# One pitch of 512 values for VectorE's exponential and term tiles, five resident w2 parts, and an order computed for loads that land later

## The chip, the cores and the metric

One core of one Trainium2 chip runs the kernel. Its time is the device time of one execution in microseconds (us). Below, PE is TensorE, DVE is VectorE, ACT is ScalarE, POOL is GpSimd and SP is SyncE, whose only work here is to issue DMAs.

## The reference

Softcap attention over 8 batches, 12 heads, 448 positions and 64 values per head is followed by a soft mixture of experts (MoE) with 8 experts of 4 slots each:

```
scores = cap * tanh((q @ k.T / 8) / cap)            # cap = 30
attn   = exp(scores - max); attn /= sum + 1e-9
x      = attn @ v  -> [3584, 768]
logits = x @ phi                                     # 32 slots
d = softmax over tokens, c = softmax over slots
slot_out[e] = relu((d.T @ x)[e] @ w1[e]) @ w2[e]     # 768 -> 1024 -> 768
out    = c @ slot_out                                # float32
```

## The kernel before

**Quads.** The 96 heads are taken four at a time, as 24 "quads"; three quads make a batch. A quad Q has 14 score tiles of 128 keys by 448 queries. They are made in six chunks of 3, 2, 3, 2, 2, 2 tiles. `SC(Q,s)` are the PE matmuls of chunk s into one of two PSUM buffers (a ring: the even chunks use the 3-bank buffer, the odd ones the 2-bank buffer). `TH(Q,s)` is the tanh of that chunk on ACT (line 526), from PSUM into SBUF. So `SC(Q,s)` can begin only when `TH` of two chunks before has read the buffer.

**Two ways to the exponential.** Tiles 0 to 7 go into `exa`; `EX(Q,0)` takes their exponential on ACT in one instruction (line 534). Tiles 8 to 13 go into `exd`; DVE makes their exponential from four integer passes `PH(Q,0..3)` (function `term`, line 541), each of which reads the tanh values as float16 and writes a bfloat16 bit pattern as uint16. The first three passes write to one of two `term` buffers in turn, the fourth writes in place to `exd`. PE adds the four patterns up by multiplying each with its own V: `PV(Q,a0)`, `PV(Q,a1)` and `PV(Q,d)` are the products with `exa`, `PV(Q,c0)` to `PV(Q,c3)` those with the four passes (function `pv_mms`, line 551).

**Around them.** `NR(Q,0)` and `NR(Q,1)` divide by the row sums on DVE (lines 584 and 585). `TX`/`CX` turn the result on PE and copy it on DVE. `T k`/`T q` turn the keys and queries on PE, `C k`/`C q` copy them on DVE. Keys arrive as float32 by SP's queue (`LK`, line 407) and are cast on DVE (`KC`, line 411). Values arrive by SP's queue in four pieces (`LV`, line 417), are cast on POOL (`VC`, line 422) and scaled on DVE (`VS`, line 425). Queries are cast in the load by POOL's queue (`L q`, line 402). Once a batch, PE makes the MoE's logits and slot sums (`LG`, `SS`, `EN`, `ET`, `ES`), with small steps on the other engines (`EE` on ACT; `ED`, `ER` on POOL; `CS`, `CE`, `CN`, `CW` on DVE).

**What sets the order.** The class `Plan` lists all these steps with an engine, a duration from the table `COST`, dependencies and a due time. The due times are moved by the table `DUE`, and `HOLD` lets a step be picked although it isn't ready for up to so many ns. `Plan.order` then plays the engines forward and writes out the order in which each engine's instructions are emitted. The engines run them in that order and wait on semaphores; nothing is reordered on the chip. In the plan a load counts as landed `COST["dma"]` ns after its transfer ends.

**The layout.** A tile of `exa` has 448 values at a pitch of `ROW` = 512. `exd` and the `term` buffers keep their six tiles in three pairs: 512 values to the second tile of a pair, and `PAIR` = 960 from one pair to the next (function `pairs`), so that one strip of 64 zeros serves both tiles of a pair. A DVE pass over six tiles therefore walks 3 pairs of 2 tiles of 448 values.

**The end.** After the attention the MoE's second layer reads w2 in 32 parts of 384 KB. `KEPT` of them stay in SBUF in bfloat16 (`w2b`). The others are cast during the attention by POOL's queue into DRAM (`w2d`, line 335) and read back by SP's queue (`w2t`, line 868) into the SBUF that the attention gives up. Matmuls of line 922 use them, line 889 is the first layer.

Of the kernel before, what the change touches and what calls it, by code (L numbers as in the profile page):

```python
# [10 lines left out]
BF16 = mybir.dt.bfloat16  # L11
U16 = mybir.dt.uint16
# [5 lines left out]
P = 128  # L18
# [3 lines left out]
S = 448  # L22
# [3 lines left out]
W = DH + 1  # L26
SLOTS = 8
ROW = 512
PAIR = ROW + S


TILES = [(0, 0, 0), (0, 1, 0), (0, None, None), (0, 0, 1), (0, 1, 1), (0, 0, 2), (0, 1, 2),
# [5 lines left out]
RQ = 2  # L38
RP = 2
ND = 6  # L40
NA = NQT - ND
# [4 lines left out]
TERMS = ((-2.18104, 1.0), (-1.928978, 1.0), (-1.674805, 0.6953125), (-1.419015, 0.6953125))  # L46
PH = len(TERMS)

DUE = {"C0k": -134148, "C0q": -266909, "CAk": -221411, "CAq": -170905, "CE": -35220, "CN": -341840, "CS": -94513,
# [7 lines left out]
HOLD = {"C0k": 61, "C0q": 1500, "CAq": 1040, "CS": 7, "CW": 892, "Ck": 1367, "Cq": 775, "ED": 657, "EE": 1500, "ET":  # L57
# [4 lines left out]
COST = dict(quad=9000, lat=200, dma=5000, form=90, sc=100, scm=200, act=0.833, act0=70, ts=0.265, ts0=70,  # L62
            pvf=31, turn=460, xturn=450, copy=610, norm=830, vcast=1060, vscale=340, kcast=560, kdiag=300,
            issue=800, load=1400, part1=2740, part2=2530, same=300)

# [1 line left out]
class Plan:  # L67
# [5 lines left out]
    def op(self, name, eng, dur, deps=(), due=0.0, take=None, give=None, after=0.0, form=(FULL, FULL), port=False):  # L73
        key = name[0] + (str(name[2]) if name[0] in ("PV", "NR", "PH", "EX", "LG", "SS") else "") + \
            (name[1] if name[0] in ("L", "X", "T", "C", "CA", "T0", "C0") else "")
        self.ops[name] = dict(name=name, eng=eng, dur=dur, deps=list(deps), due=due + DUE.get(key, 0.0),
                              key=key, hold=max(0, HOLD.get(key, 0)), take=take, give=give, after=after, form=form, port=port)

    def build(self):
        C, NQ, NQB = COST, self.NQ, self.NQB  # L80
        T = float(C["quad"])
# [108 lines left out]
    def order(self):  # L190

        ops, lat = self.ops, COST["lat"]
        engines = ("PE", "ACT", "DVE", "POOL", "SP", "DMA", "DMV")
# [8 lines left out]
        def ready(o):  # L202
            t = o["after"]
            for d in o["deps"]:
                if d not in end:
                    return None
                x = ops[d]["eng"]
                t = max(t, end[d] + (0 if x == o["eng"] else COST["dma"] if x[0:2] == "DM" else lat))
            if o["take"]:
# [5 lines left out]
        while len(end) < len(ops):  # L215
            best = None
            for e in engines:
                pick = None
                for o in todo[e][:1 if e in strict else 60]:
                    r = ready(o)  # L220
                    if r is None:
                        continue
                    late = o["due"] - (COST["same"] if e == "PE" and o["form"][0] == form else 0)
                    key = (max(r - o["hold"], free[e]), late, str(o["name"]), max(r, free[e]))
# [7 lines left out]
            if e == "PE":  # L232
                if o["form"][0] != form:
                    t = max(t, free[e] + COST["form"])
                form = o["form"][1]
# [16 lines left out]
def kernel(  # L252
# [23 lines left out]
    NQB = H // 4  # L276
    NQ = B * NQB
    NPAIR = 2 * NQ
    KEPT = 6

    ctx.enter_context(tc.manual_schedule())
    pe, dve, act, pool, sp = nc.tensor, nc.vector, nc.scalar, nc.gpsimd, nc.sync
# [30 lines left out]
           for e in range(E - 2)]  # L313
    w2b = wts.tile([P, KEPT, 4, HD], BF16, name="w2b")

# [23 lines left out]
    w2_parts = [(n0, half) for n0 in range(0, len(blocks), 4) for half in range(2)]  # L339
    w2_kept, w2_spilled = w2_parts[:KEPT], w2_parts[KEPT:]  # L340

# [7 lines left out]
    homes = {}  # L349
# [2 lines left out]
        homes[nm] = att.enter_context(tc.tile_pool(name=nm, bufs=1))  # L352
    xs = att.enter_context(tc.tile_pool(name="xs", bufs=4))
    ea = [homes[f"ea{n}"].tile([P, NA * ROW], BF16, name=f"exa{n}") for n in range(RQ)]
    ed = [homes[f"ed{n}"].tile([P, ND // 2 * PAIR], BF16, name=f"exd{n}") for n in range(RQ)]
    terms_of = [homes["tm"].tile([P, ND // 2 * PAIR], BF16, name=f"term{n}") for n in range(RP)]
    kraw = [homes["ld"].tile([P, 2, S], F32, name=f"kraw{n}") for n in range(2)]
    kcast = homes["ld"].tile([P, 2, S], BF16, name="kcast")
    vraw = [homes[f"vr{n}"].tile([P, 2, SLOTS, DH], F32, name=f"vraw{n}") for n in range(2)]
# [4 lines left out]
    def rows(t):  # L364
        return t.rearrange("p (t s) -> p t s", s=ROW)

    def pairs(t, u0, u1):

        return bass.AP(tensor=t.tensor, offset=t.offset + u0 // 2 * PAIR,
                       ap=[t.ap[0], *([[PAIR, (u1 - u0) // 2]] if u1 - u0 > 2 else []), [ROW, 2], [1, S]])  # L370

    for t in ea:
        dve.memset(rows(t)[:, :, S:ROW], 0.0)
    for t in (*ed, *terms_of):
        dve.memset(t.rearrange("p (t s) -> p t s", s=PAIR)[:, :, S:ROW], 0.0)
    for t in km:
        dve.memset(t, 0.0)
    w_low = TERMS[-1][1]
# [138 lines left out]


    def quad_ex(Q, u0, u1):
        if u1 <= NA:  # L520
            return rows(ea[Q % RQ])[:, u0:u1, 0:S]
        return pairs(ed[Q % RQ], u0 - NA, u1 - NA)

    def tanh_chunk(Q, s):
        u0, w = first_of[s], CHUNKS[s]
        act.activation(quad_ex(Q, u0, u0 + w).bitcast(F16), ring(Q, s)[:, 0:w, 0:S], ACT.Tanh,  # L526
                       scale=qk_scale / cap)

    def nd_of(Q):
        return ND_LAST if Q == NQ - 1 else ND  # L530
# [5 lines left out]
    def term_home(Q, i):  # L536
        return ed[Q % RQ] if i == PH - 1 else terms_of[(Q * (PH - 1) + i) % RP]

    def term(Q, i):
        nd = nd_of(Q)  # L540
        dve.tensor_scalar(pairs(term_home(Q, i), 0, nd).bitcast(U16),  # L541
                          quad_ex(Q, NA, NA + nd).bitcast(F16), octaves * 128, base[i], ALU.mult, ALU.add)

    def pv_mms(dst, buf, vt, tiles, begin=False, end=False):
        for g in range(NG):
            for x in tiles:
                n, a, t = TILES[x]
                for h in range(2) if a is None else (a,):
                    q0 = x * ROW if x < NA else (x - NA) // 2 * PAIR + (x - NA) % 2 * ROW
                    q0 += (g * P if not h else g * P + HP if g < NF else -HP)  # L550
                    pe.matmul(dst[:, 2 * g + h if g < NF else 2 * g, :], buf[:, q0:q0 + P],  # L551
                              vt[:, 3 + h if a is None else 5 * h + t, :],
                              start=begin, stop=end, skip_group_check=True)
                    begin = False
# [175 lines left out]
    t = wts.tile([P, 2, 2, NT, DH], BF16, name="casts", tag="w1", bufs=E)  # L730
# [32 lines left out]
    Q, bl = NQ - 1, B - 1  # L763
# [102 lines left out]
    for n0, half in sorted(w2_spilled, key=lambda x: (x[1], x[0])):  # L866
        t = tl.tile([P, 4, HD], BF16, name=f"w2t{n0}_{half}")
# [195 lines left out]
```

## Time and profile before

| what | us |
|---|---|
| median of 3 runs (302.5 to 304.14) | 303.12 |
| the profiled execution | 302.8 |
| its span, first to last instruction | 301.0 |
| PE, DVE, ACT busy in the span | 255.5, 242.0, 236.9 |
| POOL busy in the span | 99.1 |

A busy time is the union of an engine's instructions; those of neighbours overlap a little at their ends, so the distance between two starts is shorter than a duration. The attention runs to about 256 us, the experts and the output fill the rest.

### The profile page before, as it was taken

What the parts mean: (1) busy time and instruction counts of PE and PEld (TensorE: products, weight loads), DVE (VectorE), ACT (ScalarE), POOL (GpSimd) and SP (SyncE); (2) the same over time, 40 slices, a digit from 0 to 9 for tenths busy, and PEclk for the clock granted to TensorE, in tenths of its full rate; (3) what the DMA queues carried; (4) which work ended last, traced back from release to release, by engine and by line L of the source; (5) the groups of instructions that cost most, each with busy time, mean ns of one, the idle gap of its engine ahead of it and who ended that gap; (6) DMA issues with size and microseconds to landing.
All of it is one profiled execution on the core that took longest, in us unless ns stands there. A gap on an engine that the chain in (4) does not pass through costs nothing.

```text
span 301.0 us, 11981 instructions
## 1 busy us (share of the span) xinstructions
PE 255.5 (85%) x5300; PEld 188.4 (63%) x5300; DVE 242.0 (80%) x437; ACT 236.9 (79%) x207; POOL 99.1 (33%) x156
## 2 busy tenths in 40 slices
PE   4879898999898969998988899879998999998720
PEld 4357577776676758776766676668666867543300
DVE  2459898999989989999989999799989987236940
ACT  1788979999899879998988898898989896235730
POOL 3570442633352324343524341624343210300000
PEclk9999999999999999999999999999999999999995
DMA  8999999999999999999999999999989998968998
GB/s 147 271 219 222 254 255 231 250 249 244 245 239 242 245 248 240 231 229 234 233 221 191 225 208 236 160 212 227 208 185 227 233 307 285 399 264 298 404 412 332
DMA packets 58931, 74.97 MB, mean 249 GB/s; under 512 B 4864, under 2 KB 48000, under 8 KB 58880
## 3 DMA queue, kind: packets, MB, share of 16 engines
q0 software_dynamic: 30464, 30.50, 62.3%
q1 hardware_dynamic: 28256, 43.49, 44.8%
q8 instruction: 41, 0.67, 0.8%
q10 hardware_dynamic: 160, 0.23, 0.3%
q14 instruction: 10, 0.08, 0.1%
HBM read 93.68 MB, written 21.23 MB: 382 GB/s over the span
## 4 chain that ended last, share of the span: by engine, by line
PE 33%; DVE 30%; DMA 19%; issue 5%; ACT 4%; SPq 3%; POOL 1%; DVEq 0%; ACTq 0%; POOLq 0%
PE pv L551 13%; DVE term L541 12%; DMA vraw<-in_v_dram 10%; DMA kraw<-in_k_dram 5%; DVE exd L541 5%; PE sc L515 4%; DVE vw L425 3%; SPq L417 3%; DVE xq L585 3%; PE xps L596 2%; DVE kcast L411 2%; PE hp L889 2%; PE so_ps L922 2%; DMA qb<-in_q_dram 2%; PE qps L482 2%
## 5 line engine op out<-in xcount | busy, mean ns | idle before, releaser
L526 ACT ACTIVATE exa<-sc 128x1344 f16<-128x1344 f32 (+1 forms) x72 | 82.3, 1166 | 20.0 <-PE sc L512 17.4
L541 DVE TENSOR_SCALAR term<-exd 128x2688 uint16<-128x2688 f16 (+1 forms) x72 | 76.0, 1081 | 2.0 <-PE pv L551 1.1
L534 ACT ACTIVATE exa<-exa 128x3584 bf16<-128x3584 f16 x24 | 76.7, 3195 | 0.0
L526 ACT ACTIVATE exd<-sc 128x896 f16<-128x896 f32 x72 | 63.5, 918 | 5.7 <-PE sc L515 5.6
L551 PEld LDWEIGHTS <-term 128*128 128x128 bf16 x1704 | 57.5, 97 | 12.6 <-DVE term L541 7.1
L515 PE MATMUL sc<-qT,kT 64*128 64x448 bf16 x288 | 50.0, 368 | 1.9 <-ACT exa L526 1.4
L422 POOL CAST vb<-vraw 128x1024 bf16<-128x1024 f32 x24 | 25.6, 1067 | 63.8 <-PE pv L551 36.3
L551 PE MATMUL pv<-vb,term 128*128 128x65 bf16 x1136 | 43.1, 193 | 1.5 <-DVE term L541 1.2
L551 PE MATMUL pv<-vb,exa 128*128 128x65 bf16 x960 | 41.9, 196 | 1.4 <-issue 1.1
L551 PEld LDWEIGHTS <-exa 128*128 128x128 bf16 x960 | 36.3, 99 | 9.4 <-issue 6.1
L541 DVE TENSOR_SCALAR exd<-exd 128x2688 uint16<-128x2688 f16 (+1 forms) x24 | 31.0, 1290 | 0.8
L585 DVE TENSOR_TENSOR xq<-pv,rec 128x448 bf16<-128x448 f32 (+2 forms) x49 | 30.1, 615 | 1.7
L551 PE MATMUL pv<-vw,exd 128*128 128x65 bf16 x568 | 22.1, 194 | 10.6 <-DVE exd L541 8.0
L402 POOL DMA_DIRECT2D qb<-in_q_dram x23 | 16.9, 736 | 42.2 <-PE qps L482 42.2
L551 PEld LDWEIGHTS <-exd 128*128 128x128 bf16 x576 | 19.2, 97 | 13.2 <-DVE exd L541 9.8
L551 PE MATMUL pv<-vw,term 128*128 128x65 bf16 x568 | 21.8, 193 | 4.0 <-DVE term L541 3.6
L491 DVE COPY qT<-qps 128x896 bf16<-128x896 bf16 x23 | 14.2, 617 | 7.3 <-PE qps L482 6.5
L335 POOL DMA_DIRECT2D w2d<-in_moe_w_dram x26 | 19.7, 790 | 0.5 <-issue 0.5
L515 PEld LDWEIGHTS <-kT 64*128 64x128 bf16 x288 | 12.9, 93 | 10.8 <-issue 3.6
L637 POOL COPY e<-E 128x512 bf16<-128x512 bf16 x9 | 5.8, 644 | 38.8 <-PE eps L655 17.8
L331 POOL DMA_DIRECT2D w1b<-in_moe_w_dram x24 | 18.1, 756 | 0.0
L512 PE MATMUL sc<-qT,km 128*128 128x448 bf16 x48 | 18.0, 375 | 0.0
(135 smaller groups left out, 315.1 us busy)
## 6 DMA issues: line engine op xcount, KB each, us to landing
w1b<-in_moe_w_dram POOLq DMA_DIRECT2D x24, 512.0 KB, 12.1
kraw<-in_k_dram SPq DMA_DIRECT2D x23, 448.0 KB, 9.0
w2d<-in_moe_w_dram POOLq DMA_DIRECT2D x26, 384.0 KB, 9.3
w2t<-w2d SPq DMA_DIRECT2D x26, 384.0 KB, 7.4
out_dram<-ob SPq DMA_DIRECT2D x9, 768.0 KB, 6.7
vraw<-in_v_dram SPq DMA_DIRECT2D x48, 128.0 KB, 7.1
qb<-in_q_dram POOLq DMA_DIRECT2D x23, 224.0 KB, 6.7
vraw<-in_v_dram SPq DMA_DIRECT2D x48, 96.0 KB, 7.4
```

The lines of the kernel that those rows point to most:

```text
L331: pool.dma_start(out=w1b[e][:, js, :], in_=w1r[:, e, js, :])
L335: pool.dma_start(out=dst, in_=bass.AP(tensor=src.tensor, offset=src.offset + half * HD, ap=[[D, P], [F * D, 4], [1, HD]]))
L402: pool.dma_start(out=t, in_=bass.AP(tensor=srcs[nm].tensor, offset=quad_at(Q), ap=[[NT * DH, P], [2 * S * DH, 2], [1, NT * DH]]))
L422: pool.tensor_copy(vb[Q % 2][:, :, :, 0:DH], vraw[Q % 2])
L491: dve.tensor_copy(new_qkT(nm, Q), ps)
L512: pe.matmul(dst, km[Q % 2][:, n, :], qT, start=True, stop=True)
L515: pe.matmul(dst, kT[r, 2 * t:2 * t + 2, :], qT[r], start=True, stop=True)
L526: act.activation(quad_ex(Q, u0, u0 + w).bitcast(F16), ring(Q, s)[:, 0:w, 0:S], ACT.Tanh, scale=qk_scale / cap)
L534: act.activation(t, t.bitcast(F16), ACT.Exp, scale=cap)
L541: dve.tensor_scalar(pairs(term_home(Q, i), 0, nd).bitcast(U16), quad_ex(Q, NA, NA + nd).bitcast(F16), octaves * 128, base[i], ALU.mult, AL ...
L551: pe.matmul(dst[:, 2 * g + h if g < NF else 2 * g, :], buf[:, q0:q0 + P], vt[:, 3 + h if a is None else 5 * h + t, :], start=begin, stop=e ...
L585: dve.tensor_tensor(xq[Q][:, s0:s1, n, :], ps[:, s0:s1, 0:DH], rec.to_broadcast([P, s1 - s0, DH]), op=ALU.mult)
```

## The change

The six tiles of `exd` and of the `term` buffers now lie at one pitch of 512, like those of `exa`; `pairs` and `PAIR` are gone. The buffers grow from 2880 to 3072 values per partition. In return w2 keeps five parts instead of six, and 27 instead of 26 are written to DRAM and read back. `COST["dma"]` becomes 7000 instead of 5000, and `DUE` and `HOLD` have new numbers (a line of each is shown), so every engine's order is computed anew.

```diff
-DUE = {"C0k": -134148, "C0q": -266909, "CAk": -221411, "CAq": -170905, "CE": -35220, "CN": -341840, "CS": -94513,
+DUE = {"C0k": -50327, "C0q": -3265, "CAk": -29335, "CAq": -19945, "CE": -129605, "CN": 17674, "CS": -25093, "CW":
...
-HOLD = {"C0k": 61, "C0q": 1500, "CAq": 1040, "CS": 7, "CW": 892, "Ck": 1367, "Cq": 775, "ED": 657, "EE": 1500, "ET":
+HOLD = {"C0k": 688, "C0q": 1260, "CAq": 1250, "CS": 998, "CW": 685, "CX": 544, "Ck": 509, "Cq": 1290, "ED": 1500,
...
-COST = dict(quad=9000, lat=200, dma=5000, form=90, sc=100, scm=200, act=0.833, act0=70, ts=0.265, ts0=70,
+COST = dict(quad=9000, lat=200, dma=7000, form=90, sc=100, scm=200, act=0.833, act0=70, ts=0.265, ts0=70,
...
-    KEPT = 6
+    KEPT = 5
...
-    ed = [homes[f"ed{n}"].tile([P, ND // 2 * PAIR], BF16, name=f"exd{n}") for n in range(RQ)]
-    terms_of = [homes["tm"].tile([P, ND // 2 * PAIR], BF16, name=f"term{n}") for n in range(RP)]
+    ed = [homes[f"ed{n}"].tile([P, ND * ROW], BF16, name=f"exd{n}") for n in range(RQ)]
+    terms_of = [homes["tm"].tile([P, ND * ROW], BF16, name=f"term{n}") for n in range(RP)]
...
-    for t in ea:
+    for t in (*ea, *ed, *terms_of):
         dve.memset(rows(t)[:, :, S:ROW], 0.0)
-    for t in (*ed, *terms_of):
-        dve.memset(t.rearrange("p (t s) -> p t s", s=PAIR)[:, :, S:ROW], 0.0)
...
     def quad_ex(Q, u0, u1):
-        if u1 <= NA:
-            return rows(ea[Q % RQ])[:, u0:u1, 0:S]
-        return pairs(ed[Q % RQ], u0 - NA, u1 - NA)
+        t, at = (ea, 0) if u1 <= NA else (ed, NA)
+        return rows(t[Q % RQ])[:, u0 - at:u1 - at, 0:S]
...
-        dve.tensor_scalar(pairs(term_home(Q, i), 0, nd).bitcast(U16),
+        dve.tensor_scalar(rows(term_home(Q, i))[:, 0:nd, 0:S].bitcast(U16),
...
-                    q0 = x * ROW if x < NA else (x - NA) // 2 * PAIR + (x - NA) % 2 * ROW
+                    q0 = (x if x < NA else x - NA) * ROW
```

ACT, one quad in the middle of the attention, before (`exa<-sc` and `exd<-sc` are tanh chunks, `exa<-exa` is the exponential):

```order
L526 ACTIVATE exa_161<-sc_192 128x2x448
L526 ACTIVATE exa_161<-sc_191 128x3x448
L526 ACTIVATE exd_163<-sc_192 128x2x448
L534 ACTIVATE exa_161<-exa_161 128x8x448
L526 ACTIVATE exd_163<-sc_191 128x2x448
L526 ACTIVATE exd_163<-sc_192 128x2x448
```

ACT at the same place now:

```order
L517 ACTIVATE exa_162<-sc_193 128x2x448
L517 ACTIVATE exa_162<-sc_192 128x3x448
L517 ACTIVATE exd_164<-sc_193 128x2x448
L517 ACTIVATE exd_164<-sc_192 128x2x448
L525 ACTIVATE exa_162<-exa_162 128x8x448
L517 ACTIVATE exd_164<-sc_193 128x2x448
```

The exponential has moved behind the fifth tanh chunk, so that one chunk is left behind it instead of two.

DVE, the four passes over `exd` of one quad and what stands around them, before (`term<-exd` and `exd<-exd` are `PH`, `rec` and `xq` are `NR`, `kT` and `km` are `C k`, `qT` is `C q`, `xT` is `CX`, `vw` is `VS`, `kcast` is `KC`):

```order
L411 CAST kcast<-kraw_167 128x896
L541 TENSOR_SCALAR term_165<-exd_163 128x3x2x448
L541 TENSOR_SCALAR term_164<-exd_163 128x3x2x448
L584 RECIPROCAL rec<-pv 128x7
L585 TENSOR_TENSOR xq<-pv,rec 128x7x64
L541 TENSOR_SCALAR term_165<-exd_163 128x3x2x448
L541 TENSOR_SCALAR exd_163<-exd_163 128x3x2x448
L488 COPY kT<-kps 128x768
L497 COPY km_176<-kps 64x2x64 x2
```

DVE at the same place now:

```order
L532 TENSOR_SCALAR term_166<-exd_164 128x6x448
L575 RECIPROCAL rec<-pv 128x7
L576 TENSOR_TENSOR xq<-pv,rec 128x7x64
L591 COPY xT<-xps 128x896
L417 TENSOR_SCALAR vw_174<-vraw_170 128x8x64
L532 TENSOR_SCALAR term_165<-exd_164 128x6x448
L532 TENSOR_SCALAR term_166<-exd_164 128x6x448
L532 TENSOR_SCALAR exd_164<-exd_164 128x6x448
L480 COPY kT<-kps 128x768
L489 COPY km_177<-kps 64x2x64 x2
L403 CAST kcast<-kraw_167 128x896
```

The shape of a pass changes from 3x2x448 to 6x448. The division, the copy of the turned result and the scaled V now stand between the first and the second pass, and the cast of the keys stands behind the key copies, a quad ahead of where it stood. On PE (too long to show row by row) all six score chunks of the next quad now stand ahead of `PV(Q,c1)` to `PV(Q,c3)`, where the last two stood behind them; in most quads the turn of the keys stands between chunks 4 and 5, and the score groups of a quad number six instead of five.

More of the change, by code (lines that the diff above doesn't have):

```diff
@@ L28 @@
 ROW = 512
-PAIR = ROW + S
 TILES = [(0, 0, 0), (0, 1, 0), (0, None, None), (0, 0, 1), (0, 1, 1), (0, 0, 2), (0, 1, 2),
@@ L365, in rows @@
         return t.rearrange("p (t s) -> p t s", s=ROW)
-    def pairs(t, u0, u1):
-        return bass.AP(tensor=t.tensor, offset=t.offset + u0 // 2 * PAIR,
-                       ap=[t.ap[0], *([[PAIR, (u1 - u0) // 2]] if u1 - u0 > 2 else []), [ROW, 2], [1, S]])
-    for t in ea:
+    for t in (*ea, *ed, *terms_of):
         dve.memset(rows(t)[:, :, S:ROW], 0.0)
-    for t in (*ed, *terms_of):
-        dve.memset(t.rearrange("p (t s) -> p t s", s=PAIR)[:, :, S:ROW], 0.0)
     for t in km:
```

22 rows, old and new, of tables (DUE, HOLD) are left out of this document.

## The prediction

> **What bounds the kernel now.** First the span and clock of the core, then busy time by stretches: start, first four quads, the steady attention, experts and output.
>
> ```profile
> core 0: 301.0 us, clock 0.987
> core 0: us, PE busy (x) PEld busy (x) DVE busy (x) ACT busy (x) POOL busy (x), PEclk, DMA share, GB/s
> 20.00:56.00 36.00, 32.37 (x665) 24.13 (x665) 32.51 (x54) 30.36 (x25) 13.76 (x16) 1.00 1.13 241
> 56.00:250.00 194.00, 176.47 (x3973) 136.97 (x3969) 178.19 (x309) 175.33 (x142) 72.30 (x101) 1.00 1.13 230
> 163.70:173.80 10.10, 8.84 (x202) 6.97 (x201) 9.81 (x17) 8.84 (x8) 3.95 (x6) 1.00 1.13 210
> 171.10:182.10 11.00, 10.84 (x255) 8.66 (x253) 10.70 (x20) 10.18 (x10) 5.88 (x9) 1.00 1.19 228
> ```
>
> Then the timeline of ACT, for the pace: the big exponential `exa<-exa` comes once a quad. The rows are those of quads 0, 4, 12, 13 and 23, and the tanh chunks between 12 and 13.
>
> ```profile
> 14.45 3.19 ACT L534 ACTIVATE exa<-exa 128x3584 bf16<-128x3584 f16 x1
> 56.73 3.20 ACT L534 ACTIVATE exa<-exa 128x3584 bf16<-128x3584 f16 x1
> 126.91 3.19 ACT L534 ACTIVATE exa<-exa 128x3584 bf16<-128x3584 f16 x1
> 129.99 1.73 ACT L526 ACTIVATE exd<-sc 128x896 f16<-128x896 f32 x2
> 131.89 2.10 ACT L526 ACTIVATE exa<-sc 128x1344 f16<-128x1344 f32 x2 [0.18 <-PE sc L512]
> 134.22 1.29 ACT L526 ACTIVATE exa<-sc 128x1344 f16<-128x1344 f32 x1 [0.22 <-PE sc L512]
> 135.40 0.91 ACT L526 ACTIVATE exd<-sc 128x896 f16<-128x896 f32 x1
> 136.20 3.19 ACT L534 ACTIVATE exa<-exa 128x3584 bf16<-128x3584 f16 x1
> 247.42 3.19 ACT L534 ACTIVATE exa<-exa 128x3584 bf16<-128x3584 f16 x1
> ```
>
> From 56.73 to 247.42 lie 19 periods: (247.42 - 56.73)/19 = 10.04 us a quad. The first four take (56.73 - 14.45)/4 = 10.57. Over 56 to 250 us the engines' loads, scaled to 10.04 us, are DVE 178.19/194 x 10.04 = 9.22, PE 9.13, ACT 9.07. So three engines are within 2% of each other, DVE is the fullest, and 10.04 - 9.22 = 0.82 us a quad is lost to their waiting for each other. The two short stretches show who holds the pace where: from 163.7 to 173.8 DVE has 9.81 of 10.10 us and PE 8.84; in 171.1 to 182.1, where the MoE step of a batch lies, PE has 10.84 of 11.00.
>
> Where ACT loses time the waits of the whole span tell:
>
> ```profile
> ACT exa L526 <- PE sc L512: 17.4, 22, 2.3
> ACT exd L526 <- PE sc L515: 5.6, 11, 1.1
> ```
>
> These are mostly a quad's first chunk. Its scores go into the buffer that the fifth tanh chunk must first have read, and behind that tanh ACT has only one short chunk left (the 1.73 of two at 129.99 is chunks 4 and 5).
>
> **The passes of DVE.** The row that decides is the length of a pass over `exd`. Six tiles and four tiles both occur, the latter in the last quad:
>
> ```profile
> L541 DVE TENSOR_SCALAR term<-exd 128x2688 uint16<-128x2688 f16 x69 | 74.3, 1101 | 1.8 <-PE pv L551 0.9 <-ACT exd L526 0.7
> L541 DVE TENSOR_SCALAR exd<-exd 128x2688 uint16<-128x2688 f16 x23 | 30.3, 1319 | 0.8
> 243.45 2.08 DVE L541 TENSOR_SCALAR term<-exd 128x2688 uint16<-128x2688 f16 x2 [0.67 <-ACT exd L526]
> 246.22 1.08 DVE L541 TENSOR_SCALAR term<-exd 128x2688 uint16<-128x2688 f16 x1
> 251.50 1.15 DVE L541 TENSOR_SCALAR term<-exd 128x1792 uint16<-128x1792 f16 x2
> 252.87 0.63 DVE L541 TENSOR_SCALAR term<-exd 128x1792 uint16<-128x1792 f16 x1 [0.22 <-PE pv L551]
> ```
>
> Two six-tile passes take 2.08 us together, one alone 1.08, so a second starts 2.08 - 1.08 = 1.00 after the first. For four tiles it is 1.15 - 0.63 = 0.52. Six tiles at the rate of four would be 0.52 x 6/4 = 0.78. They take 0.22 more. Both shapes have a third dimension, so that can't be the reason; what differs is the count of pairs, three against two. [...]
>
> [...]
>
> [...] Four passes a quad save 4 x 0.22 = 0.88, and DVE's load falls from 9.22 to 8.34.
>
> **The order.** *ACT:* one chunk of tanh moves ahead of the exponential. The next quad's first scores may start when the fifth tanh is read, and now 3.08 us of exponential (126.91 to 129.99) lie behind that instead of 0.8. The wait for the first chunk should go; the 0.2 us waits of the third chunk (131.89, 134.22) stay. *PE:* the last two score chunks no longer stand behind `PV(Q,c1)` to `PV(Q,c3)`, which wait for DVE's passes, so ACT isn't starved by a late pass. The price is a sixth score group. Its size shows here:
>
> ```profile
> 133.52 0.36 PE L515 MATMUL sc<-qT,kT 64*128 64x448 bf16 x2
> 133.82 0.36 PE L512 MATMUL sc<-qT,km 128*128 128x448 bf16 x1
> 139.46 0.55 PE L515 MATMUL sc<-qT,kT 64*128 64x448 bf16 x4
> 139.94 0.58 PE L482 MATMUL qps<-ident,qb 128*64 128x128 bf16 x14
> 140.85 0.90 PE L551 MATMUL pv<-vb,exa 128*128 128x65 bf16 x24
> ```
>
> Four tiles in one group hold PE 0.48 us (139.46 to 139.94), two tiles 0.30 (133.52 to 133.82), so two groups cost 0.12 more. I take 0.10 a quad, bounds 0 and 0.2. PE's load becomes 9.23. The exponential ends 0.81 later (one two-tile tanh, half of the 1.73 at 129.99 less the overlap). Its first reader on PE starts at 140.85, and the exponential of 136.20 ends at 139.39: 1.46 us of slack, which covers it. *DVE:* the cast of the next keys moves a quad ahead; behind it wait the second division and the next quad's first pass. The load it needs is issued a quad earlier too, since the cast of two quads before frees its buffer.
>
> **The period.** After the change PE (9.23) is the fullest, then ACT (9.07), then DVE (8.34). Of the 0.82 lost before I keep half, 0.41: the waits of ACT for the first chunk and of PE for late passes go, while the MoE step of each third quad, where PE had 10.84 of 11.00, stays and PE can't be faster there. That is 9.64 us a quad, 0.40 less. Bounds: 9.33 if only 0.10 is lost, 10.05 if all 0.82 stays.
>
> **The small edits.** The 27th part is one more load in the row that brings w2 back:
>
> ```profile
> 238.00 24.44 SPq L868 DMA_DIRECT2D w2t<-w2d  x24
> L868 SPq DMA_DIRECT2D w2t<-w2d x26: 319/320/1412, 226.9 to 262.0; - x26
> DMA to landing us min/median/max: 2.9/7.4/8.6
> 272.09 1.48 PE L922 MATMUL so_ps<-w2t,hpad 128*32 128x384 bf16 x32
> 6.08 0.46 DVE L454 CAST casts<-raw 128x256 bf16<-128x256 f32 x2 [3.91 <-DMA raw<-in_q_dram]
> 1.42 0.24 DVE L375 MEMSET exd<- 128x96 uint32 x2
> ```
>
> 24 loads take 24.44 us, so one more is 1.02 us. The last was issued at 262.0 and lands by 262.0 + 8.6 = 270.6; its matmuls are the last of the 32 that start at 272.09 and end at 273.57. One more load lands by 271.6, still ahead of them: nothing, or 1.0 if that cover is gone. The larger memsets add about 0.1 for each of four tiles (0.24 for two now); DVE then waits 3.91 us for the first load, so nothing.
>
> **The sum**, against the profiled execution (302.8 us, of which 301.0 is the span):
> - 19 steady periods x 0.40 = 7.6
> - four starting periods x 0.2 = 0.8. I take half the steady gain, since loads and the empty pipeline hold them.
> - the end of the attention, where four six-tile passes of quad 22 stand before the last division: 0.88 at most; I take 0.3, since ACT's last chunks end nearly as late.
>
> Together 8.7: 302.8 - 8.7 = 294.1. The median of the runs is 0.3 above the profiled execution, so I predict 294.4 us. Best end of the bounds: 19 x 0.71 + 4 x 0.4 + 0.9 = 16.0, which gives 287.1.
>
> **Rivals.**
>
> *1. PE waits for the later exponential (slower).* PE runs in order, and `PV(Q,a0)` waits for an exponential that ends 0.81 later. If PE reaches it with no other work in front, its 9.23 becomes 10.04, and with 0.2 of other waits 10.24, against 10.04 now: 23 x 0.20 = 4.6, thus 303.1 + 4.6 = 307.7 us. It decides once PE stands idle over 0.8 us ahead of that product in a normal quad. For it: PE is now the fullest engine, and the scores stand ahead of everything. Against it: the slack of 1.46 us, and that the first scores of the next quad and the turn of the queries stand before that product. Chance 0.11.
>
> *2. The pitch changes nothing on DVE (no change).* Then DVE stays at 9.22, and only the order acts; with 0.78 to 0.82 lost the period is 10.00 to 10.04, about 302.3 us. Against it stand 1.00 and 0.52. Chance 0.03.
>
> *3. The loads hold the pace (no change).*
>
> ```profile
> HBM read 93.68 MB, written 21.23 MB: 382 GB/s over the span
> PE qps L482 <- DMA qb<-in_q_dram: 3.4, 2, 2.0
> POOL vb L422 <- DMA vraw<-in_v_dram: 12.9, 3, 7.5
> ```
>
> For it: the DMA share is 1.13 through the attention. Against it: PE and POOL wait for loads only in a few places, and the share reaches 1.19 in the stretch from 171.1. If it holds, a quad stays at 10.04: 302.3 us. Chance 0.04.
>
> **How the numbers follow.** The forecast has 0.82, the rivals 0.11, 0.03 and 0.04. About 0.5%, 1.5 us, is what a measurement can tell here. Faster by more: 0.82. Within: the two rivals of no change, 0.07. Slower: 0.11. The range runs from 288, just inside the best end, to 302, which leaves out the slower rival, most of the others, and a little below: under 2 in 10.
>
> **What would show it.** In the changed profile a six-tile pass should take about 0.85 us (0.78 from start to start) instead of 1.08, DVE's busy time fall by about 92 x 0.22 = 20 us to 222, ACT's wait for the first chunk fall from 17.4 to below 8, and the exponentials follow at about 9.64 us. PE should be the fullest engine of the steady attention. The prediction is wrong if passes still take 1.08, if PE's wait ahead of `pv<-vb,exa` grows to most of a microsecond a quad, or if the waits for `kraw`, `vraw` and `qb` grow by as much as DVE gains.

## The result, and the profile after

The changed kernel takes 299.7 us (median of 9 runs, 297.16 to 301.73) beside 303.71 us for the kernel before on the same chip: a ratio of 0.9859, 95% interval [0.9815, 0.9902]. It is faster by 1.4%; the forecast was 2.9%. The direction and the range held, the size did not. The medians here and below count every run, the ratios only the undisturbed ones.

The profiled execution took 297.8 us. Its span, then busy time in the stretches that the prediction used, and in the two halves of the attention; the last two rows are the same halves of the kernel before. The last three columns are PE's granted clock, the DMA share and the GB/s moved.

```profile
core 0: 296.0 us, clock 0.958
20.00:56.00 36.00, 34.28 (x747) 25.95 (x747) 29.80 (x56) 34.72 (x29) 17.42 (x21) 0.98 1.13 240
56.00:250.00 194.00, 178.09 (x4033) 138.00 (x4029) 161.25 (x314) 172.39 (x142) 77.99 (x99) 1.00 1.15 240
53.00:146.00 93.00, 83.41 (x1860) 63.94 (x1861) 75.88 (x149) 81.15 (x68) 41.41 (x52) 1.00 1.16 242
146.00:232.00 86.00, 81.17 (x1849) 63.01 (x1845) 75.90 (x146) 79.86 (x66) 37.26 (x48) 1.00 1.18 226
```

```profile
53.00:146.00 93.00, 84.84 (x1905) 65.67 (x1906) 86.75 (x150) 83.91 (x70) 37.20 (x52) 1.00 1.15 240
146.00:232.00 86.00, 77.30 (x1739) 59.96 (x1739) 78.84 (x138) 76.73 (x62) 34.00 (x47) 1.00 1.13 210
```

DVE is no longer full: 161.25 of 194 us where it had 178.19. But PE has hardly filled up, 178.09 after 176.47. In the first half PE is even busy less than before (83.41 of 93 us, before 84.84); only in the second half does it gain, from 77.30 to 81.17 of 86 us. The transfers show the same split: in the first half they moved 240 GB/s before and 242 now; in the second 210 before and 226 now.

The pace, from ACT's timeline: the exponentials of quads 0, 4, 13 and 22 after the change, and of quads 13 and 22 before it.

```profile
15.00 3.20 ACT L525 ACTIVATE exa<-exa 128x3584 bf16<-128x3584 f16 x1
52.87 3.21 ACT L525 ACTIVATE exa<-exa 128x3584 bf16<-128x3584 f16 x1
145.77 3.18 ACT L525 ACTIVATE exa<-exa 128x3584 bf16<-128x3584 f16 x1
232.44 3.18 ACT L525 ACTIVATE exa<-exa 128x3584 bf16<-128x3584 f16 x1
```

```profile
146.95 3.19 ACT L534 ACTIVATE exa<-exa 128x3584 bf16<-128x3584 f16 x1
238.60 3.20 ACT L534 ACTIVATE exa<-exa 128x3584 bf16<-128x3584 f16 x1
```

| us a quad | before | after |
|---|---|---|
| quads 0 to 4 | 10.57 | 9.47 |
| quads 4 to 13 | 10.02 | 10.32 |
| quads 13 to 22 | 10.18 | 9.63 |
| quads 4 to 22 together | 10.10 | 9.98 |

The forecast of 9.64 came true in one half of the steady attention and failed in the other. The span fell by 5.0 us: 4 x 1.10 = 4.4 in the first four quads, 18 x 0.13 = 2.3 in quads 4 to 22, less 0.8 in the last period (8.82 before, 9.63 now), 0.55 for a later first exponential and 0.35 for a longer end.

The passes and ACT's waits for scores, by groups and by the waits of the span:

```profile
L532 DVE TENSOR_SCALAR term<-exd 128x2688 uint16<-128x2688 f16 x69 | 59.8, 888 | 1.9 <-PE pv L542 1.2 <-ACT exd L517 0.5
L532 DVE TENSOR_SCALAR exd<-exd 128x2688 uint16<-128x2688 f16 x23 | 19.8, 860 | 0.8
91.66 1.62 DVE L532 TENSOR_SCALAR term<-exd 128x2688 uint16<-128x2688 f16 x2
89.14 0.85 DVE L532 TENSOR_SCALAR term<-exd 128x2688 uint16<-128x2688 f16 x1
ACT exa L517 <- PE sc L507: 10.9, 11, 2.3
ACT exa L517 <- PE sc L504: 9.8, 16, 1.5
```

Two passes take 1.62 us and one 0.85, so the second starts 0.77 after the first, where it was 1.00. ACT's wait in the row of the first chunk (L504, before L512; the third chunk is in that row too) has fallen from 17.4 to 9.8, while that for the second chunk (L507) has risen from 2.2 to 10.9. With the 5.6 before and 0.5 now of the chunks of `exd`, all of ACT's waits for scores fell only from 25.2 to 21.2.

Loads come late too, but they did so before. First the shares of the chain that ended last, before and then after:

```profile
PE 33%; DVE 30%; DMA 19%; issue 5%; ACT 4%; SPq 3%; POOL 1%; DVEq 0%; ACTq 0%; POOLq 0%
```

```profile
PE 58%; DMA 15%; DVE 11%; issue 5%; ACT 3%; POOL 2%; SPq 1%; DVEq 0%; ACTq 0%; POOLq 0%
```

DVE's share went over to PE. Behind the first query load, five loads stood on the chain before (46.9 us together) and three stand there now (35.8). Here are those three (start, length), then what happened around one of them:

```profile
58.93 13.22 DMA vraw<-in_v_dram
122.80 16.60 DMA qb<-in_q_dram
209.18 6.00 DMA vraw<-in_v_dram
```

```profile
122.80 1.00 POOL L394 DMA_DIRECT2D qb<-in_q_dram  x1 [5.00 <-PE sc L507]
139.44 0.58 PE L474 MATMUL qps<-ident,qb 128*64 128x128 bf16 x14 [2.03 <-DMA qb<-in_q_dram]
140.07 0.62 DVE L483 COPY qT<-qps 128x896 bf16<-128x896 bf16 x1 [2.34 <-PE qps L474]
141.45 0.92 ACT L517 ACTIVATE exa<-sc 128x896 f16<-128x896 f32 x1 [2.28 <-PE sc L507]
```

A load of queries is issued at 122.80 and lands 16.6 us later, behind w2 loads on the same queue (the three issued from 113.9 to 117.0 us took 19.1 to 21.4 us to land). PE waits 2.03 us for it; the scores that stand behind it in PE's order come late as well, and ACT waits 2.28 us for them. Landing times over the span, before and then after (the last number of a row is the median in us):

```profile
w1b<-in_moe_w_dram POOLq DMA_DIRECT2D x24, 512.0 KB, 12.1
qb<-in_q_dram POOLq DMA_DIRECT2D x23, 224.0 KB, 6.7
```

```profile
w1b<-in_moe_w_dram POOLq DMA_DIRECT2D x24, 512.0 KB, 14.7
qb<-in_q_dram POOLq DMA_DIRECT2D x23, 224.0 KB, 10.4
HBM read 94.08 MB, written 21.63 MB: 391 GB/s over the span
```

### The profile page after: what moved, and what is told of

Same layout as the page of the kernel before. It is cut to its first block, busy times and chain, and to the rows that moved or that the text cites. A ratio compares the mean times of both kernels' runs of the same rounds, so it can differ in the third digit from the quotient of the medians.

```text
span 296.0 us, 11975 instructions
## 1 busy us (share of the span) xinstructions
PE 254.1 (86%) x5300; PEld 186.1 (63%) x5300; DVE 219.7 (74%) x437; ACT 235.1 (79%) x207; POOL 107.6 (36%) x156
## 2 busy tenths in 40 slices
DMA packets 59075, 75.37 MB, mean 255 GB/s; under 512 B 4880, under 2 KB 48016, under 8 KB 59024
## 3 DMA queue, kind: packets, MB, share of 16 engines
HBM read 94.08 MB, written 21.63 MB: 391 GB/s over the span
## 4 chain that ended last, share of the span: by engine, by line
PE 58%; DMA 15%; DVE 11%; issue 5%; ACT 3%; POOL 2%; SPq 1%; DVEq 0%; ACTq 0%; POOLq 0%
PE pv L542 26%; PE sc L507 9%; DMA qb<-in_q_dram 8%; DMA vraw<-in_v_dram 6%; PE sc L504 3%; PE xps L587 3%; PE qps L474 3%; DVE term L532 2%; PE hp L880 2%; PE so_ps L913 2%; PE kps L474 2%; PE op L1005 2%; DVE kcast L403 1%; DMA raw<-in_q_dram 1%; DVE ob L1012 1%
## 5 line engine op out<-in xcount | busy, mean ns | idle before, releaser
L517 ACT ACTIVATE exa<-sc 128x1344 f16<-128x1344 f32 (+1 forms) x72 | 83.1, 1170 | 21.2 <-PE sc L507 10.9
L542 PEld LDWEIGHTS <-term 128*128 128x128 bf16 x1704 | 55.7, 97 | 12.6 <-issue 8.0
L532 DVE TENSOR_SCALAR term<-exd 128x2688 uint16<-128x2688 f16 (+1 forms) x72 | 61.6, 877 | 1.9 <-PE pv L542 1.2
L507 PE MATMUL sc<-qT,kT 64*128 64x448 bf16 x288 | 53.0, 369 | 2.6 <-ACT exa L517 0.9
L542 PE MATMUL pv<-vb,exa 128*128 128x65 bf16 x960 | 38.7, 193 | 4.1 <-issue 3.3
L542 PEld LDWEIGHTS <-exa 128*128 128x128 bf16 x960 | 33.6, 97 | 10.2 <-issue 7.8
L394 POOL DMA_DIRECT2D qb<-in_q_dram x23 | 18.9, 823 | 53.6 <-PE sc L507 27.8
L507 PEld LDWEIGHTS <-kT 64*128 64x128 bf16 x288 | 13.9, 93 | 14.7 <-issue 5.2
L417 DVE TENSOR_SCALAR vw<-vraw 128x512 bf16<-128x512 f32 x24 | 12.3, 512 | 13.1 <-PE pv L542 9.0
L334 POOL DMA_DIRECT2D w2d<-in_moe_w_dram x27 | 21.3, 804 | 1.3 <-issue 0.8
L532 DVE TENSOR_SCALAR exd<-exd 128x2688 uint16<-128x2688 f16 (+1 forms) x24 | 20.4, 850 | 0.8
L591 DVE COPY xT<-xps 128x896 bf16<-128x896 bf16 x23 | 14.3, 622 | 7.2 <-PE xps L587 7.0
## 6 DMA issues: line engine op xcount, KB each, us to landing
qb<-in_q_dram POOLq DMA_DIRECT2D x23, 224.0 KB, 10.4
```

The costliest lines, as they stand in the source:

```text
L334: pool.dma_start(out=dst, in_=bass.AP(tensor=src.tensor, offset=src.offset + half * HD, ap=[[D, P], [F * D, 4], [1, HD]]))
L394: pool.dma_start(out=t, in_=bass.AP(tensor=srcs[nm].tensor, offset=quad_at(Q), ap=[[NT * DH, P], [2 * S * DH, 2], [1, NT * DH]]))
L507: pe.matmul(dst, kT[r, 2 * t:2 * t + 2, :], qT[r], start=True, stop=True)
L532: dve.tensor_scalar(rows(term_home(Q, i))[:, 0:nd, 0:S].bitcast(U16), quad_ex(Q, NA, NA + nd).bitcast(F16), octaves * 128, base[i], ALU.mu ...
L591: dve.tensor_copy(xTs[Q], held.pop(("x", Q)))
```

## The experiments

The theory to be tested, L: after the change the attention is held by the transfers, not by DVE or PE; what DVE saves goes into waiting for loads. Rivals: D, DVE and the order set the pace and the gain is merely smaller; E, one part of the change undoes the other.

| kernel | median us | ratio to before, 95% interval |
|---|---|---|
| changed | 299.70 | 0.9859 [0.9815, 0.9902] |
| new layout, old order | 302.45 | 0.9940 [0.9899, 0.9980] |
| old layout, new order | 299.36 | 0.9872 [0.9819, 0.9924] |
| before, W loads halved | 296.95 | 0.9787 [0.9738, 0.9836] |
| new layout, old order, W loads halved | 286.70 | 0.9449 [0.9397, 0.9500] |
| changed, W loads halved | 285.54 | 0.9421 [0.9374, 0.9468] |
| changed, w2 loads halved | 293.03 | 0.9671 [0.9629, 0.9713] |
| changed, w1 loads halved | 290.39 | 0.9591 [0.9541, 0.9640] |
| changed, four kept parts | 299.21 | 0.9856 [0.9813, 0.9899] |
| the same with a third query buffer | 299.96 | 0.9889 [0.9854, 0.9923] |
| old layout, dimensions exchanged, new order | 297.98 | 0.9839 [0.9790, 0.9888] |
| changed, loads spread by 6% | 297.70 | 0.9816 [0.9773, 0.9859] |
| dimensions exchanged, loads spread by 6% | 297.88 | 0.9802 [0.9760, 0.9845] |
| changed, loads even by bytes | 297.83 | 0.9828 [0.9784, 0.9873] |
| dimensions exchanged, loads even by bytes | 296.87 | 0.9796 [0.9752, 0.9839] |

Each ratio is to the kernel before on the same chip. W loads are those of w1 and w2.

**One part at a time.** The new layout with the tables of before (`DUE`, `HOLD`, `COST`), and the old layout with the new tables.

```diff
 # new layout, old order
-COST = dict(quad=9000, lat=200, dma=7000, form=90, sc=100, scm=200, act=0.833, act0=70, ts=0.265, ts0=70,
+COST = dict(quad=9000, lat=200, dma=5000, form=90, sc=100, scm=200, act=0.833, act0=70, ts=0.265, ts0=70,
...
 # old layout, new order
-COST = dict(quad=9000, lat=200, dma=5000, form=90, sc=100, scm=200, act=0.833, act0=70, ts=0.265, ts0=70,
+COST = dict(quad=9000, lat=200, dma=7000, form=90, sc=100, scm=200, act=0.833, act0=70, ts=0.265, ts0=70,
...
```

> The new layout (one pitch, five resident parts) with the old order (old DUE, HOLD and 5000). Theory L (late loads eat half of what DVE frees): the passes take 0.86 us instead of 1.08, DVE is idle by 20 us more, but the old order still has its own late loads and its scores behind the late passes: 299 to 302 us, so the pitch alone brings most of the 4 us. Rival O (the new order costs what the pitch gains): 294 to 297 us, faster than the changed kernel. Rival N (the pitch needs the new order): 303 us.

> The old layout (pairs, six resident parts) with the new order (new DUE, HOLD and 7000). Theory L: DVE's passes stay at 1.08 us and DVE stays the fullest engine, 302 to 305 us, no gain from the order alone. Rival O: 305 to 309 us, slower than before, since the order itself costs. If the order is the gain: 300 us.

The layout alone gave 0.6%, the order alone 1.3%, both 1.4%: on the new order the faster passes added nothing that these runs can tell. Both expectations from L missed: 299 to 302 for the layout, which gave 302.45, and 302 to 305 for the order, which gave 299.36. Yet the passes were as fast as after the change in the one and as slow as before in the other. Groups of the new layout with the old order, then of the old layout with the new:

```profile
L532 DVE TENSOR_SCALAR term<-exd 128x2688 uint16<-128x2688 f16 x69 | 59.6, 889 | 10.3 <-PE pv L542 10.2
```

```profile
L541 DVE TENSOR_SCALAR term<-exd 128x2688 uint16<-128x2688 f16 x69 | 75.5, 1120 | 1.2 <-PE pv L551 0.7 <-ACT exd L526 0.5
```

With the old order DVE's saved time turns up as waiting: 10.3 us of idle time ahead of the passes, 10.2 of it for PE to have read a `term` buffer. In that trace the faster passes shorten quads 13 to 22 alone (10.18 us before, 9.70 now), where the kernel before moves 210 GB/s. Quads 0 to 4 (10.57 and 10.94) and 4 to 13 (10.02 and 10.16), where it moves 239 in both, get no shorter.

**Half the bytes of W.** Every load of w1 and w2 moves half its values, on the changed kernel, on the kernel before and on the new layout with the old order.

```diff
-        pool.dma_start(out=w1b[e][:, js, :], in_=w1r[:, e, js, :])
+        pool.dma_start(out=w1b[e][:, 2 * jh:2 * jh + 1, :], in_=w1r[:, e, 2 * jh:2 * jh + 1, :])
...
-        pool.dma_start(out=dst, in_=bass.AP(tensor=src.tensor, offset=src.offset + half * HD,
-                                            ap=[[D, P], [F * D, 4], [1, HD]]))
+        pool.dma_start(out=dst[:, 0:2, :], in_=bass.AP(tensor=src.tensor, offset=src.offset + half * HD,
+                                            ap=[[D, P], [F * D, 2], [1, HD]]))
...
```

> The changed kernel with the weight loads of POOL's queue (w1 and w2, issued during the attention) at half their bytes, as many instructions as before; the experts then use each loaded half twice, and the loads that bring w2 back keep their bytes. Theory L: the late loads of q and v go (q lands in 6 us instead of 10.4), no period of a quad is over 10.5 us, and the time is 288 to 292 us. Rival P (PE and its order hold the pace, the loads only look late): 297 to 300 us.

> The kernel before with the same halved weight loads. Theory L: DVE holds the pace at 9.65 us a quad (the best three periods of before took 28.96), the few late loads go: 295 to 298 us, so halved loads bring this kernel less than the changed one. Rival P: 303 us, nothing.

> The new layout with the old order, with halved weight loads as in the two kernels before it (285.5 us with the new order, 297.0 with old layout and old order). It shows how much of those 11.4 us is the pitch once the loads leave room. Theory L: the pitch is worth as much as the forecast gave both together once the loads are light, 288 to 292 us. Rival Q (even then it is the order that counts): 294 to 297 us.

With the transfers relieved the layout is worth 296.95 - 286.70 = 10.3 us, where with all bytes it was worth 303.75 - 302.45 = 1.3 on the old order and nothing that shows on the new. The order then adds 286.70 - 285.54 = 1.2, which the intervals don't separate; the old layout with the new order and half the bytes wasn't run. So the faster passes are worth more than the prediction's whole sum (8.7, at best 16.0) once the loads are lighter. Both kernels with the new layout came out below L's 288 to 292 us; the kernel before, 296.95, lies in its range. Rivals P and Q are ruled out. On the changed kernel with half the bytes the quads from 4 to 22 take 9.29 us, and the rows of the halves are:

```profile
53.00:146.00 93.00, 89.95 (x2054) 69.69 (x2051) 83.65 (x163) 89.01 (x74) 41.17 (x57) 1.00 0.93 191
146.00:232.00 86.00, 82.14 (x1891) 64.14 (x1889) 76.72 (x148) 82.56 (x67) 33.68 (x45) 1.00 0.87 185
```

PE has 89.95 of 93 us in the first half instead of 83.41. With the same instructions in the same order on every engine, half of W's bytes bring the changed kernel 14 us: D is ruled out, and the bytes of W hold back what the passes save.

How they do it is a second question. The table splits a quad, from exponential to exponential, into PE's busy time and its idle time by what ended that (us a quad, from the windows and PE's waits between these exponentials; terms under 0.1 left out):

| kernel, quads | period | PE busy | idle until DVE | until a load | no cause in the profile |
|---|---|---|---|---|---|
| before, 4 to 13 | 10.02 | 9.14 | 0.57 | 0.16 | 0.10 |
| changed, 4 to 13 | 10.32 | 9.24 | 0.14 | 0.24 | 0.70 |
| changed, W halved, 4 to 13 | 9.34 | 9.04 | 0.10 | none | 0.18 |
| before, 13 to 22 | 10.18 | 9.22 | 0.53 | none | 0.40 |
| changed, 13 to 22 | 9.63 | 9.09 | 0.16 | none | 0.31 |
| changed, W halved, 13 to 22 | 9.24 | 8.97 | 0.28 | none | none |

PE's waits for DVE went as the prediction said. What came in their place in quads 4 to 13 is mostly idle time that the profile gives no cause for, and only to a small part a wait for a load. Half the bytes take most of both away. So L holds in its first part (the transfers), while its second part, that the time goes into waiting for late loads, is shown for 0.24 us a quad only (0.16 before).

**Which half, which load.** In the changed kernel w1's loads are issued from 13 to 99 us, w2's from 107 to 226; quad 13 begins at 146. So w2 and w1 were halved apart, each with the edit above for itself.

> The changed kernel with half the bytes in every load of w2, and w1 whole; the output is not the reference's, for half of w2's values are repeated. w1's loads fall into about the first half of the attention, w2's into the second. Theory L (the loads hold the pace): periods stay near 9.9 us in quads 4 to 11 and fall to about 9.3 in quads 13 to 22; the time is 292 to 294 (10 periods x 0.6 = 6 us off 299.5). Rival (another thing about the half loads, such as the MLP stage, gave the gain): periods stay at 9.9 in both halves and the time moves by more or less than that in the stage behind the attention.

> The changed kernel with half the bytes in every load of w1, and w2 whole; the output is not the reference's, for half of w1's values are repeated. The complement of the run with w2 halved. Theory L: quads 4 to 13 fall from 10.32 to about 9.5, quads 13 to 22 stay at 9.6; the time is 290 to 292. Rival (the first half is held by something else than w1's bytes): quads 4 to 13 stay above 10, the time at 297 to 300.

Quads 4 to 13 took 10.17 us with w2 halved and 9.71 with w1 halved; quads 13 to 22 took 9.26 and 9.31. Quads 4 to 11, the stretch of w1, take 10.02 in the changed kernel, 10.06 with w2 halved and 9.42 with w1 halved. Both times, 293.03 and 290.39, lie in L's ranges. Loads on the chain that ended last, with w2 halved, behind the first query load:

```profile
60.44 13.26 DMA vraw<-in_v_dram
77.11 11.73 DMA vraw<-in_v_dram
95.34 14.41 DMA qb<-in_q_dram
```

With w1 halved, the only one between the start and the output:

```profile
202.42 6.07 DMA vraw<-in_v_dram
```

Whichever weight is whole puts late loads on the chain in its own stretch, and nowhere else. Two parts of the expectation missed with w1 halved: quads 4 to 13 came to 9.71, not about 9.5, and quads 13 to 22 should have stayed at 9.6 and came to 9.31, at 234 GB/s there. What carries over from the first half into the second wasn't traced.

**Depth or rate.** Is a query load late because it is issued late? Four kept w2 parts make room for a third buffer; the control has the four parts alone.

```diff
-    KEPT = 5
+    KEPT = 4
...
-        t = homes["ld"].tile([P, 2, S], BF16, name=nm + "b", tag=nm + "raw", bufs=2)
+        t = homes["ld"].tile([P, 2, S], BF16, name=nm + "b", tag=nm + "raw", bufs=3)
```

> The changed kernel with four resident w2 parts instead of five: one more part of 0.75 MB is read and cast into DRAM during the attention and read back. Theory L by rate: each part is 0.4 MB written and 0.4 MB more read of about 116 MB, so 0.7% or 1 to 2 us: 300.5 to 302 us. Rival S: no difference, 299.7 us.

> The changed kernel with three buffers instead of two for the q and k loads that share a tag, paid for by four kept w2 parts instead of five (that alone gave 299.2 us). POOL can issue q loads a buffer earlier. Theory R (the bytes a second of the transfers hold the pace): the transfers stay as full, so the stalls shift and the time stays at 298.5 to 299.5. Rival Q (a load is issued too late for its landing time, and depth would hide it): qb's waits at PE's transposes go, 294 to 297. POOL's waits for a qb buffer should fall in both.

299.96 us against 299.21, not faster: rival Q is ruled out. The control missed L's 300.5 to 302 us; one more part cost nothing that shows, though 1 us would lie within the intervals. POOL's waits in the control, then with three buffers:

```profile
POOL qb L394 <- PE sc L507: 27.5, 6, 7.4
POOL qb L394 <- PE qps L474: 26.0, 11, 5.4
POOL vb L414 <- DMA vraw<-in_v_dram: 20.0, 6, 6.5
```

```profile
POOL qb L394 <- PE sc L507: 0.6, 1, 0.6
POOL vb L414 <- DMA vraw<-in_v_dram: 44.8, 10, 8.8
```

The wait for a buffer is gone, 27.5 + 26.0 us of it, and the wait for the values' load, which POOL now reaches earlier, has grown from 20.0 to 44.8. PE's wait for queries fell from 4.5 to 2.6 us, but the query loads took longer to land (median 11.8 us, in the control 10.4), and no time was won. Here a deeper buffer is no cure.

**Is it the odd count?** The old paired tiles, with the two outer dimensions of a pass exchanged: 2 x 3 x 448 in place of 3 x 2 x 448; new order, six kept parts.

```diff
-                       ap=[t.ap[0], *([[PAIR, (u1 - u0) // 2]] if u1 - u0 > 2 else []), [ROW, 2], [1, S]])
+                       ap=[t.ap[0], [ROW, 2], *([[PAIR, (u1 - u0) // 2]] if u1 - u0 > 2 else []), [1, S]])
```

> The old layout (pairs, six resident parts) with the new order, and in the DVE passes the two outer dimensions change places: 2 of 3 of 448 instead of 3 of 2 of 448, so the outermost count is even without the wider pitch. If the odd count is the reason for the slow pass, the passes take 0.86 us; if it is the pair layout as such, 1.08. Time by theory L: between 297.5 and 299.7 us, that is the changed kernel without its 27th trip of a w2 part, since DVE is no longer what holds the pace. Rival D (DVE's passes hold the pace where the loads don't): under 296 us.

```profile
L541 DVE TENSOR_SCALAR term<-exd 128x2688 uint16<-128x2688 f16 x69 | 60.1, 892 | 1.4 <-PE pv L551 0.8 <-ACT exd L526 0.5
```

892 ns, as fast as the one pitch (888), on the same addresses as the 1101 before and the 1120 of the same order without the exchange: the outermost count decides here, not the pitch. With three the pass is slow, with two or six it isn't; three is the only odd count of these passes, and by what way it slows them no trace shows. The kernel time, 297.98, lies in L's range and below the changed kernel's, and this kernel needs no larger buffers and no further part of w2 in DRAM; the intervals overlap, so that difference isn't shown.

**Moving the loads, with all bytes.** In the list that `Plan.order` gives, the 56 W loads are put at other places: spread over 6% more of the list, or so that their bytes are even from the first to the last. The lines here are those of the spreading.

```diff
...
+    order = list(rest)
+    for r, nm in reversed(at_w):
+        order.insert(min(len(rest), int(at_w[0][0] + (r - at_w[0][0]) * 1.06)), nm)
```

> The changed kernel with the 56 weight loads of POOL's queue spread over 6% more of the attention, everything else in the same order on every engine. Theory L by rate (the loads fill the DMA engines, and fewer bytes per us in the attention let q, k and v land earlier): 296 to 298.5 us. Rival S (the loads are late by their place in POOL's queue, not by the rate): 299 to 301 us. A weight that arrives too late for the experts would show as more than 301.

> The old paired tiles with their two outer dimensions exchanged (2 x 3 x 448 instead of 3 x 2 x 448), six kept w2 parts, the new order, and the 56 W loads spread over 6% more of the attention. Theory L (the loads hold the pace): both edits alone gave 297.7 and 298.0 us; the swap frees DVE's time but that time goes into late loads, the spreading takes a little of the loads' pressure away, so the two together should give 296 to 297.5. Rival E (both take away the same wait): no better than either alone, 297.5 to 298.5. Rival D (DVE was the pace and the spreading is chance): 298 to 299.

> The changed kernel with its 56 W loads placed so that the bytes are even from the first to the last of them; nothing else moves. Theory L in its sharper form (the transfers have a ceiling of about 243 GB/s in the attention, and only where they stand at it do quads stay long): the load of 53 to 146 us falls and that of 146 to 232 us rises towards 240 GB/s; quads 4 to 13 come to 9.9 to 10.1 instead of 10.32, quads 13 to 22 to 9.6 to 9.8; the time is 296 to 298, against 299.7. Rival (the place of the loads doesn't matter, another thing holds the first half): quads 4 to 13 stay at 10.3 and the time at 299 to 300.

> The old paired tiles with their two outer dimensions exchanged, six kept w2 parts, the new order, and the W loads evened out by bytes. Theory L: as the changed kernel with the loads evened out, less a spilled part, 295.5 to 297.5. Rival: as the exchange alone, 298.

All four lie between 296.87 and 297.88 us, about 2 to 3 below the changed kernel, but their intervals overlap with its own: the gain is likely, not shown. Spreading on top of the exchange (0.9802 against 0.9839 and 0.9816 alone) doesn't tell L's sum from rival E. In the changed kernel with its loads spread, the loads that bring w2 back take 8.7 us to land in the median (5.7 without the spreading), and the time from the last exponential to the end grows from 53.9 to 55.1 us. The traces say more. The halves of the changed kernel with the bytes even:

```profile
53.00:146.00 93.00, 85.22 (x1889) 65.31 (x1885) 76.27 (x147) 82.41 (x70) 38.69 (x50) 0.98 1.12 236
146.00:232.00 86.00, 80.74 (x1837) 62.48 (x1831) 74.48 (x145) 79.64 (x65) 39.76 (x51) 1.00 1.23 236
```

The rates are now equal, the query loads land in 6.6 us (median), as fast as in the kernel before (6.7), and from 20 us on no load stands on the chain any more. Still the quads take 10.18 in the first half (9.9 to 10.1 was expected) and 9.67 in the second. So late loads are not what holds the pace there. Of the first half's 10.18 PE is busy for 9.32 and idle for 0.83 without a cause that the profile shows; more on that below. The best of the runs with whole loads, 296.87 us, is the exchange with even loads: 2.0% under the kernel before.

## Why the prediction was wrong in size

- **The passes.** Right. 0.77 from start to start (0.78 forecast), DVE's busy time 219.7 us on the page (222 forecast), and the outermost count of three shown as the reason (1120 ns, with two 892). That six tiles at one pitch would run at the rate of four was the author's estimate (0.52 x 6/4); by what way the count acts no run shows. The fourth, in-place pass gained more than the others (1319 to 860 ns in the mean), which the sum, with 0.22 for each of the four, hadn't counted.
- **The order.** Right in its sign, and underrated. ACT's first-chunk wait fell to 9.8, not to below 8, and what it lost came back as the wait for the second chunk (2.2 to 10.9). With all bytes the order alone gives 1.3%, as much as both. The later exponential did not hold PE: its idle time ahead of `pv<-vb,exa` is 4.1 us over the whole span (before 1.4), not most of a microsecond a quad, and the slower rival did not come about.
- **The period.** This step failed: "Of the 0.82 lost before I keep half, 0.41". PE became the fullest engine, and its busy time came out near the forecast (9.17 us a quad in quads 4 to 22, 9.23 forecast), but it stands idle for 0.81 and not 0.41: 1.08 in quads 4 to 13, 0.54 in quads 13 to 22. The waits that were to go did go, PE's for DVE from 0.57 to 0.14 and from 0.53 to 0.16. In quads 4 to 13 others took their place: 0.24 for loads (0.16 before) and 0.70 without a cause in the profile (0.10 before). With half of W's bytes 0.18 is left of these 0.94 us. So the step put at nothing what the transfers take from PE once DVE no longer does; by what way they take the 0.70 stays open. The term 19 x 0.40 = 7.6 measured 1.5: 2.3 in quads 4 to 22, less 0.8 in the last period.
- **What else was off in the period.** I took the old loss as the engines' waiting for each other, and a part of it was the transfers too: halved loads alone shorten a quad of the kernel before from 10.10 to 9.87. And 0.82 was the loss beside DVE; beside PE, which was to hold the pace, it was 10.04 - 9.13 = 0.91. That quads 13 to 22 took 9.63, close to the 9.64, is partly luck (9.09 and 0.54 instead of 9.23 and 0.41).
- **The loads as a rival.** It was given 0.04, on the ground that PE and POOL waited for loads in few places. That reads what waits now, not what would wait next. The page of the kernel before had loads at 19% of the chain that ended last, and the transfers moved 240 GB/s from 53 to 146 us with DVE as the fullest engine (242 now). Neither was used, and the row of 382 GB/s was quoted and not used. The rival's own time, 302.3, was wrong as well, since quads 0 to 4 and 13 to 22 did get shorter.
- **The start.** Four periods x 0.2 = 0.8 was forecast, 4.4 came: 10.57 fell to 9.47 a quad. It takes both parts: 10.94 with the layout alone, 10.18 with the order alone. Most of the 5.0 us thus comes from a place where the prediction expected little, which is luck. The rate there is 239 GB/s before and now, so the shorter quads carry fewer bytes, 2.26 MB instead of 2.53 (period x rate); quads 4 to 13 carry more, 2.50 MB instead of 2.40, and 16 of w1's loads are issued in them instead of 13. What quads 0 to 4 gained, quads 4 to 13 in part gave back. This fits L, but no run held the places of the loads while the rest of the order changed.
- **The small edits.** The 27th part shows no wait: its time from last exponential to end of span is 53.9 us (before 53.6). The end of the attention brought no 0.3; the last period, counted above, grew by 0.8.

The prediction named its own failure: waits for `kraw`, `vraw` and `qb` that grow by as much as DVE gains. POOL's wait for `vraw` went from 12.9 to 15.1 and PE's for `qb` from 3.4 to 4.1, far less than the 22 us off DVE. The sign did not show although the loads did take the gain, since PE's pauses name no load. The periods and the halved loads showed it.

## What to carry to other kernels

When an engine that is 92% full is relieved, set the transfers beside the next engine stretch by stretch. Here the stretch that already moved 240 GB/s got no shorter (10.02 to 10.32 us a quad), and the one at 210 did (10.18 to 9.63), whatever waits for loads the profile showed. The first four quads, at 239, did get shorter, but with fewer bytes in them. To find out how much of a gain the loads will swallow, halve their bytes in both versions and compare the change there with the change at full bytes (here 10.3 us against 1.3). And try the outer dimensions of a DVE pass in the other order: exchanging a count of three and one of two in its access pattern took it from 1120 to 892 ns here without moving any data.

## What the runs showed of the hardware

- **The rate in the attention.** In no half of the attention, of any kernel run with whole loads, did the transfers move more than 243 GB/s, while slices of the stage behind it reach 413 (the page's row of the changed kernel, 40 slices):

```profile
GB/s 159 276 224 242 234 260 235 245 248 230 250 246 237 242 248 247 254 244 223 235 248 232 219 235 241 157 225 245 243 209 228 236 307 346 390 206 310 408 413 306
```

  The W and query loads are cast from four bytes to two on their way, so the bytes read are more than the row counts (75.37 MB moved on that page, 94.08 MB read from HBM). Taken from the HBM row less what is read back and written at the end (27 parts of 0.39 MB and 11.0 MB), the attention and what precedes it move 94.1 MB in about 250 us: an estimate of 376 GB/s, in which a cast from DRAM to DRAM counts as read and as written. What sets the lower rate in the attention no run shows.

- **PE pauses that the profile gives no cause for shrink with the bytes of the loads.** In the waits of PE's matmuls from 56 to 230 us they show as "issue". The kernel before:

```profile
PE pv L551 <- DVE exd L541: 6.2, 8, 1.1
PE pv L551 <- issue: 3.7, 7, 1.0
PE pv L551 <- DVE term L541: 2.8, 6, 0.6
```

  The changed kernel, the same with half of W's bytes, and with even bytes:

```profile
PE pv L542 <- issue: 5.4, 8, 1.3
PE sc L504 <- issue: 1.5, 1, 1.5
```

```profile
PE pv L542 <- issue: 1.8, 2, 1.2
```

```profile
PE pv L554 <- issue: 9.4, 16, 1.1
PE sc L516 <- issue: 2.0, 1, 2.0
```

  All lines together, it is 4.5 us before, then 8.7, 2.8 and 12.7. The instructions of the changed kernel and of that with half the bytes are the same and in the same order, so the transfers make that difference. The rate alone doesn't set the pauses: at 242 and 226 GB/s in the halves of the attention the changed kernel has 8.7, that with even bytes, at 236 in both, 12.7, and the old layout with the new order, at 243 and 226, 5.2. By what way they arise no run shows; it stays open.
